# Retention into a gated FFN on one core: state casts two groups behind their block, one chunk's load behind the down weights, three blocks for chunks 4 to 7, and a longer run of half-column ups

## The chip, the cores and the metric

One core of a Trainium2 chip. The metric is the device time of one execution in microseconds (us). The fast executions of one kernel lie within 1% of each other, mostly within 0.7%; a few fall in a slower state, and they are left out. The kernel before took 236.76 us (median of 3, 236.72 to 236.99). Kernels are timed in rounds beside the kernel before, in sessions, each on one chip of its own.

## The reference, cut to what matters

```python
# retention: 4 batches, 8 heads, 768 tokens, head size 64; a decay gamma per head
state = gamma * state + outer(k[t], v[t])
y[t]  = scale * q[t] @ state
x     = y as 3072 tokens x 512
# gated FFN, d_ff = 1536
out = (sigmoid(x @ w_gate) * (x @ w_val)) @ w_out
```

The kernel cuts each batch into six chunks of 128 tokens (24 chunks in all) and the tokens of the FFN into six tiles of 512, which are four chunks each.

## The kernel before

TensorE (PE) is fed from one program order. The FFN of a tile is a list of groups: twelve `up` groups (gate and value matmuls, 512 columns), then eight half `down` groups. `plan` puts retention work between the groups: `step_t` transposes a chunk, `block(done, new)` finishes two chunks and starts two. In the code, `kn`, `qn` and `vf` are the loaded k, q and v of a chunk, `zbd` is the state in bf16, and `wg`, `wv` and `wo` are the gate, value and down weights. A bank is one of the seven PSUM buffers that PE's results go to; the program reuses it when another engine has read it out. "First columns" below are the first matmuls on columns 256 to 511 of tile 1.

```python
pf = ctx.enter_context(tc.tile_pool(name="pf", bufs=7, space=bass.MemoryType.PSUM))   # rotating banks
...
def state_sum(g):                       # g, g + 1: VectorE sums, then the casts on ScalarE
    ...
        nc.vector.tensor_tensor(new_za(g), za[g - 1], z[:, 0], op=ALU.add)
        state_out(g, za[g])             # two ScalarE copies: fp32 state to bf16 zbd
    if c + 1 < NCH - 1:
        nc.vector.tensor_tensor(new_za(g + 1), za[g], z[:, 1], op=ALU.add)
        state_out(g + 1, za[g + 1])

def step_t(g):
    transposes(g)                       # PE needs kn, qn; ScalarE copies the bank out
    scale_v(g, nc.vector)               # needs vf

def block(done, new):
    ...
    for g in olds: inter(g)             # PE: y from the state (needs zbd of g - 1)
    for g in news: scores(g)            # PE: two PSUM banks per chunk
    for g in olds: intra(g)             # PE: y from the masked scores
    ...                                 # PE: state(g) of the new chunks
    for g in olds: y_out(g)             # VectorE: y * decay -> xT, which the ups read
    for g in news: masks(g)             # VectorE: two masks per chunk free its score banks
    if news:
        state_sum(new)

def down(t, sm, part):
    ...
    ob = ffn.tile([128, D_MODEL], F32, tag="ob", name="ob")     # the pool has 3 buffers
    nc.scalar.copy(ob, o)
    nc.sync.dma_start(out=out[row:row + 128, :], in_=ob)
...
load_chunk(4)
for s in range(4): load_out(s)          # down weights
for g in range(5, 8): load_chunk(g)
...
plan = {
    0: [(4, step_t, 4), (10, step_t, 5), (11, block, None, 4), (11, step_t, 6), (13, step_t, 7), (14, block, 4, 6)],
    1: [(2, step_t, 8), (5, step_t, 9), (7, block, 6, 8), (12, step_t, 10), (14, step_t, 11), (15, block, 8, 10),
        (20, block, 10, None)],
    ...
}
# tile 1: eight ups on columns 0..255 (chunks 4, 5), then these ups' columns 256..511 (chunks 6, 7)
groups[:8] = [lambda n1=n1: up(1, n1, 0, 256) for n1 in range(8)]
groups[8:8] = [lambda n1=n1: up_columns(1, range(n1, n1 + 2), 256, 512) for n1 in range(0, 8, 2)]
```

Of the kernel before, what the change touches and what calls it, by code (L numbers as in the profile page):

```python
# [17 lines left out]
def kernel(  # L18
# [15 lines left out]
    NCH = S // C  # L34
# [25 lines left out]
    def load_v(g, eng):  # L60
        vf[g] = ld.tile([C, H, D], F32, tag="vf", name="vf", bufs=8)
        eng.dma_start(out=vf[g], in_=src(v, g))  # L62

    def load_kq(g):
        kn[g] = ld.tile([C, H, D], BF16, tag="kn", name="kn")
        qn[g] = ld.tile([C, H, D], BF16, tag="qn", name="qn")
        nc.gpsimd.dma_start(out=kn[g], in_=src(k, g))  # L67
        nc.gpsimd.dma_start(out=qn[g], in_=src(q, g))  # L68

    def load_chunk(g):  # L70
        load_kq(g)
        load_v(g, nc.gpsimd)
# [64 lines left out]
    zz, za = {}, {}  # L137
# [34 lines left out]
    def scores(g):  # L172
        t = qkT[g]
        sc[g] = (bank([128, NP, C]), bank([128, NP, C]))
        for p in range(NP):
            for i in range(2):
                half = slice(i * D, (i + 1) * D)
                nc.tensor.matmul(sc[g][i][:, p, :], t[half, p, :], t[half, NP + p, :], start=True, stop=True)  # L178
# [7 lines left out]
    def inter(g):  # L186
        y[g] = bank([128, NP, C])
        if g % NCH > 0:
            for p in range(NP):
                nc.tensor.matmul(y[g][:, p, :], zbd[(g - 1) % 4][:, p, :], qkT[g][:, NP + p, :],  # L190
                                 start=(p == 0), stop=False, skip_group_check=True)

    def state(g, to, start, stop=True):
        for p in range(NP):
            for i in range(2):
                nc.tensor.matmul(to[i * D:(i + 1) * D, p, :], kn[g][:, 2 * p + i, :], vs[g][:, 2 * p + i, :],
                                 start=start, stop=stop, skip_group_check=True)

    def state_out(g, z):
        for i in range(2):  # L200
            half = slice(i * D, (i + 1) * D)
            nc.scalar.copy(zbd[g % 4][half, :, half], z[half])  # L202
# [11 lines left out]
    def new_za(g):  # L214
        za[g] = at.tile([128, NP, D], F32, tag="za", name="za", bufs=3)
        return za[g]

    def state_sum(g):
        c = g % NCH
        z = zz[g]  # L220
        if c == 0:
            state_out(g, z[:, 0])
            nc.vector.tensor_copy(new_za(g), z[:, 0])
        else:
            nc.vector.tensor_tensor(new_za(g), za[g - 1], z[:, 0], op=ALU.add)  # L225
            state_out(g, za[g])
        if c + 1 < NCH - 1:
            nc.vector.tensor_tensor(new_za(g + 1), za[g], z[:, 1], op=ALU.add)
            state_out(g + 1, za[g + 1])

    def intra(g):
        first = g % NCH == 0
        for p in range(NP):
            for i, st in enumerate((stA[g], stB[g])):
                nc.tensor.matmul(y[g][i * D:(i + 1) * D, p, :], vs[g][:, 2 * p + i, :], st[:, p, :],  # L235
                                 start=(first and p == 0), stop=True, skip_group_check=True)

    def y_out(g):
        c = g % NCH
        if g % 4 == 0:  # L240
            xT[g // 4] = at.tile([128, NP, 512], BF16, tag="xT", name="xT")
        col = (g % 4) * C
        nc.vector.tensor_tensor(xT[g // 4][:, :, col:col + C], y[g], taby[:, :, c * C:(c + 1) * C], op=ALU.mult)  # L243
# [5 lines left out]
    def block(done, new):  # L249

        olds = [] if done is None else [done, done + 1]
        news = [] if new is None else [new, new + 1]
        for g in olds:
            inter(g)
        for g in news:
            scores(g)
        for g in olds:
            intra(g)
        if news:
            zz[new] = pz.tile([128, 2, NP, D], F32, tag="z", name="z")  # L260
            for i, g in enumerate(news):
                if g % NCH < NCH - 1:
                    state(g, zz[new][:, i], True)
        for g in olds:
            y_out(g)
        for g in news:
            masks(g)
        if news:
            state_sum(new)


# [2 lines left out]
    def up(t, n1, lo=0, hi=512):  # L274
        if t not in hT:
            hT[t] = ffn.tile([128, NFF, 512], BF16, tag="hT", name="hT", bufs=2)
        ps = []
        for w in (wg, wv):
            u = bank([128, 512])
            for kk in range(KT):  # L280
                nc.tensor.matmul(u[:, lo:hi], w[:, kk, n1 * 128:(n1 + 1) * 128], xT[t][:, kk, lo:hi],  # L281
                                 start=(kk == 0), stop=(kk == KT - 1))
            ps.append(u)
        gs = ffn.tile([128, 512], F32, tag="gs", name="gs")
        nc.scalar.activation(gs[:, lo:hi], ps[0][:, lo:hi], AX.Sigmoid)  # L285
        nc.vector.tensor_tensor(hT[t][:, n1, lo:hi], gs[:, lo:hi], ps[1][:, lo:hi], op=ALU.mult)  # L286

    def up_columns(t, n1s, lo, hi):
        n = hi - lo
        ps = []  # L290
        for w in (wg, wv):
            u = bank([128, 512])
            for i, n1 in enumerate(n1s):
                for kk in range(KT):
                    nc.tensor.matmul(u[:, i * n:(i + 1) * n], w[:, kk, n1 * 128:(n1 + 1) * 128], xT[t][:, kk, lo:hi],  # L295
                                     start=(kk == 0), stop=(kk == KT - 1))
            ps.append(u[:, :len(n1s) * n])
        gs = ffn.tile([128, 512], F32, tag="gs", name="gs")
        g = gs[:, :len(n1s) * n]
        nc.scalar.activation(g, ps[0], AX.Sigmoid)  # L300
        nc.vector.tensor_tensor(hT[t][:, n1s[0]:n1s[-1] + 1, lo:hi], g.rearrange("p (i n) -> p i n", n=n),
                                ps[1].rearrange("p (i n) -> p i n", n=n), op=ALU.mult)
# [55 lines left out]
    for s in range(2, NFF // 2):  # L358
        load_gate_val(s)
    extend_taby(512, 768)  # L360
    load_chunk(4)
    for s in range(4):
        load_out(s)
    for g in range(5, 8):
        load_chunk(g)
    keep_on(8)
    scores(0)
# [45 lines left out]
    def downs(t):  # L413
        return [lambda sm=sm, i=i: down(t, sm, i) for sm in range(4) for i in range(2)]

    plan = {
        0: [(4, step_t, 4), (10, step_t, 5), (11, block, None, 4), (11, step_t, 6), (13, step_t, 7), (14, block, 4, 6)],
        1: [(2, step_t, 8), (5, step_t, 9), (7, block, 6, 8), (12, step_t, 10), (14, step_t, 11), (15, block, 8, 10),
            (20, block, 10, None)],
        2: [(1, block, None, 12), (7, block, 12, 14), (15, block, 14, 16)],  # L420
        3: [(6, block, 16, 18), (15, block, 18, 20)],
        4: [(6, block, 20, 22), (14, block, 22, None)],
        5: [],
    }
    for t in range(NT):
        groups = ups(t) + downs(t)
        if t == NT - 1:
            groups[-2:] = [lambda: last_down(t)]
        if t == 0:
            groups = groups[4:]  # L430
            for g in range(8, 12):
                load_chunk(g)
        if t == 1:
            groups[:8] = [lambda n1=n1: up(1, n1, 0, 256) for n1 in range(8)]
            groups[8:8] = [lambda n1=n1: up_columns(1, range(n1, n1 + 2), 256, 512) for n1 in range(0, 8, 2)]
            for g in range(12, 16):
                load_chunk(g)
        if t == 2:
            scale_v(14, nc.gpsimd)
            scale_v(15, nc.gpsimd)  # L440
            load_chunk(18)
            scale_v(16, nc.gpsimd)
            scale_v(17, nc.gpsimd)
            load_chunk(19)
        if t == 3:
            for g in range(18, 22):
                scale_v(g, nc.gpsimd)
            load_chunk(22)
            load_chunk(23)
            scale_v(22, nc.gpsimd)  # L450
            scale_v(23, nc.gpsimd)
        for i, group in enumerate(groups):
            if i == len(groups) - 9:
                for g in range(4 * t + 8, 4 * t + 12):
                    if XBAR <= g < NG:
                        xbar(g)
            if t == 1 and i == len(groups) - 4:
                scale_v(12, nc.gpsimd)
                scale_v(13, nc.gpsimd)
                load_chunk(16)  # L460
                load_chunk(17)
            if t == 2 and i == len(groups) - 4:
                load_chunk(20)
                load_chunk(21)
            group()
            for at_group, step, *g in plan[t]:
                if at_group == i:
                    step(*g)
# [30 lines left out]
```

## Time and profile before

| view of the kernel before | reading |
|---|---|
| span of the profiled run | 235.7 us, PE busy 224.2 |
| VectorE (DVE), ScalarE (ACT) busy | 109.6 and 90.1 us |

The prediction shows four waits of PE, which it calls A to D. What stood behind the longest of them, C, is this stretch of the DVE timeline (start, length, engine, line, operation, count, idle before and what ended it):

```profile
55.15 1.29 DVE L243 TENSOR_TENSOR xT<-ff,taby 128x512 bf16<-128x512 f32 x2 [1.54 <-PE ff L235]
56.36 0.68 DVE L183 TENSOR_TENSOR stA<-ff,causal 128x512 bf16<-128x512 f32 x1
...
58.75 0.41 DVE L223 COPY za<-z 128x256 f32<-128x256 f32 x1
59.20 0.42 DVE L228 TENSOR_TENSOR za<-za,z 128x256 f32<-128x256 f32 x1
```

The block of chunks 4 and 6 gives DVE two y products, four masks and two sums, 4.5 us of work. The casts on ACT need the sums, which come last, and were put into ACT's queue at the block itself, so everything ACT owed PE stood behind them until 60.5 us.

### The profile page before, as it was taken

Reading aid. Unit: us, or ns where it says so; the run is one execution under the profiler, and the core shown is the slowest. Engines: PE = TensorE matmul, PEld = TensorE weight load, DVE = VectorE, ACT = ScalarE, POOL = GpSimd, SP = SyncE. Lnnn points to the kernel's source line nnn. Section 1 sums busy time; section 2 is a strip of 40 time slices with the busy share of each in tenths; the row PEclk is TensorE's granted clock in tenths of the full one; section 3 lists DMA queues with packets and bytes.
Section 4 is the critical chain, followed back from the end, with each engine's and each line's share of the span. In section 5 each row is a group of like instructions: output and inputs, shape, how many; then the busy total and the mean of one; then the engine's idle time right before and its main releaser. Section 6 shows DMA issues by size and latency. Waiting matters only on the chain.

```text
span 235.7 us, 4436 instructions
## 1 busy us (share of the span) xinstructions
PE 224.2 (95%) x1786; PEld 124.5 (53%) x1786; DVE 109.6 (46%) x200; ACT 90.1 (38%) x176; POOL 92.3 (39%) x111
## 2 busy tenths in 40 slices
PE   6879999899789999999999999999999999999994
PEld 6655644357678555444545445445445444444444
DVE  4566444077676473075844335735345722234301
ACT  8755334253726423245061432420632521333211
POOL 8999766588888543395013730000000000000000
PEclk9999999999999999999999999999999999999999
DMA  8999999999999999999999994002200001200022
GB/s 145 183 185 165 197 205 205 192 241 215 197 196 137 107 110 144 211 140 107 94 125 135 149 213 86 0 1 92 90 0 3 0 19 72 89 0 0 0 92 89
DMA packets 77556, 27.29 MB, mean 116 GB/s; under 512 B 65056, under 2 KB 73120, under 8 KB 77536
## 3 DMA queue, kind: packets, MB, share of 16 engines
q0 software_dynamic: 57616, 16.78, 81.3%
q1 hardware_dynamic: 19776, 10.16, 23.7%
q8 instruction: 14, 0.23, 0.4%
q10 hardware_dynamic: 144, 0.07, 0.1%
q14 instruction: 6, 0.05, 0.1%
HBM read 28.31 MB, written 6.29 MB: 147 GB/s over the span
## 4 chain that ended last, share of the span: by engine, by line
PE 77%; DMA 9%; POOL 8%; DVE 2%; issue 1%; ACT 0%; POOLq 0%; DVEq 0%
PE ff L281 40%; PE ff L312 24%; DMA wo<-in_moe_w_out_dram 5%; DMA wg<-in_moe_w_gate_dram 5%; PE ff L295 3%; PE ff L178 2%; PE ff L235 2%; PE ff L190 2%; POOL wg L81 2%; POOL wv L81 2%; PE ff L149 2%; POOL vf L62 1%; PE ff L332 1%; POOL qn L68 1%; POOL vs L169 1%
## 5 line engine op out<-in xcount | busy, mean ns | idle before, releaser
L286 DVE TENSOR_TENSOR hT<-gs,ff 128x512 bf16<-128x512 f32 (+2 forms) x72 | 45.7, 649 | 72.6 <-PE ff L281 57.4
L281 PE MATMUL ff<-xT,wg 128*128 128x512 bf16 (+2 forms) x288 | 69.7, 365 | 0.7 <-DVE xT L243 0.7
L281 PE MATMUL ff<-xT,wv 128*128 128x512 bf16 (+2 forms) x288 | 69.7, 365 | 0.0
L312 PE MATMUL ff<-wo,hT 128*128 128x512 bf16 x276 | 62.1, 380 | 1.2 <-DMA wo<-in_moe_w_out_dram 1.2
L285 ACT ACTIVATE gs<-ff 128x512 f32<-128x512 f32 (+2 forms) x72 | 39.5, 569 | 44.0 <-PE ff L281 43.5
L281 PEld LDWEIGHTS <-wv 128*128 128x128 bf16 x288 | 28.1, 98 | 29.9 <-DMA wv<-in_moe_w_val_dram 0.3
L312 PEld LDWEIGHTS <-hT 128*128 128x128 bf16 x276 | 26.4, 98 | 32.2 <-issue 1.6
L281 PEld LDWEIGHTS <-wg 128*128 128x128 bf16 x288 | 27.4, 98 | 28.3 <-issue 0.7
L317 ACT COPY ob<-ff 128x512 f32<-128x512 f32 x23 | 13.4, 585 | 38.3 <-PE ff L312 33.9
L243 DVE TENSOR_TENSOR xT<-ff,taby 128x512 bf16<-128x512 f32 x24 | 15.6, 687 | 24.9 <-PE ff L235 24.9
L202 ACT CAST zbd<-za 64x256 bf16<-64x256 f32 x26 | 10.5, 403 | 43.4 <-DVE za L225 33.9
L169 POOL TENSOR_TENSOR vs<-vf,tabv 128x512 bf16<-128x512 f32 x14 | 14.7, 1056 | 31.3 <-PE ff L281 12.9
L62 POOL DMA_DIRECT2D vf<-in_v_dram x23 | 21.1, 916 | 6.8 <-DMA kn<-in_k_dram 2.3
L67 POOL DMA_DIRECT2D kn<-in_k_dram x23 | 21.0, 914 | 3.6 <-DMA wo<-in_moe_w_out_dram 1.4
L68 POOL DMA_DIRECT2D qn<-in_q_dram x23 | 20.5, 890 | 3.1 <-DMA wo<-in_moe_w_out_dram 2.2
L183 DVE TENSOR_TENSOR stA<-ff,causal 128x512 bf16<-128x512 f32 x24 | 16.4, 682 | 3.4 <-PE ff L178 3.3
L184 DVE TENSOR_TENSOR stB<-ff,causal 128x512 bf16<-128x512 f32 x24 | 16.3, 681 | 0.0
L169 DVE TENSOR_TENSOR vs<-vf,tabv 128x512 bf16<-128x512 f32 x10 | 7.4, 736 | 7.6 <-DMA vf<-in_v_dram 7.6
L151 ACT ACTIVATE qkT<-ff 128x1024 bf16<-128x1024 bf16 x8 | 8.2, 1030 | 4.4 <-PE ff L149 4.3
L324 PE MATMUL ff<-ident 128*128 128x128 bf16 x82 | 7.3, 254 | 1.6 <-POOL ident masks.py:199 1.6
L235 PE MATMUL ff<-stA,vs 128*64 128x128 bf16 x96 | 8.2, 222 | 0.5 <-DVE stA L183 0.5
L235 PE MATMUL ff<-stB,vs 128*64 128x128 bf16 x96 | 7.9, 222 | 0.4 <-DVE stB L184 0.4
(62 smaller groups left out, 138.2 us busy)
## 6 DMA issues: line engine op xcount, KB each, us to landing
vf<-in_v_dram POOLq DMA_DIRECT2D x23, 256.0 KB, 7.9
out_dram<-ob SPq DMA_DIRECT2D x23, 256.0 KB, 3.3
kn<-in_k_dram POOLq DMA_DIRECT2D x23, 128.0 KB, 7.9
qn<-in_q_dram POOLq DMA_DIRECT2D x23, 128.0 KB, 7.8
wg<-in_moe_w_gate_dram POOLq DMA_DIRECT2D x6, 256.0 KB, 7.3
wv<-in_moe_w_val_dram POOLq DMA_DIRECT2D x6, 256.0 KB, 7.8
wo<-in_moe_w_out_dram POOLq DMA_DIRECT2D x4, 384.0 KB, 10.4
kf<-in_k_dram SPq DMA_DIRECT2D x1, 256.0 KB, 3.2
```

The lines of the kernel that those rows point to most:

```text
L62: eng.dma_start(out=vf[g], in_=src(v, g))
L67: nc.gpsimd.dma_start(out=kn[g], in_=src(k, g))
L68: nc.gpsimd.dma_start(out=qn[g], in_=src(q, g))
L169: eng.tensor_tensor(vs[g], vf[g], tabv[:, g % NCH, :].unsqueeze(2).to_broadcast([C, H, D]), op=ALU.mult)
L183: nc.vector.tensor_tensor(stA[g], sc[g][0], causal4, op=ALU.mult)
L184: nc.vector.tensor_tensor(stB[g], sc[g][1], causal4, op=ALU.mult)
L235: nc.tensor.matmul(y[g][i * D:(i + 1) * D, p, :], vs[g][:, 2 * p + i, :], st[:, p, :], start=(first and p == 0), stop=True, skip_group_che ...
L243: nc.vector.tensor_tensor(xT[g // 4][:, :, col:col + C], y[g], taby[:, :, c * C:(c + 1) * C], op=ALU.mult)
L281: nc.tensor.matmul(u[:, lo:hi], w[:, kk, n1 * 128:(n1 + 1) * 128], xT[t][:, kk, lo:hi], start=(kk == 0), stop=(kk == KT - 1))
L285: nc.scalar.activation(gs[:, lo:hi], ps[0][:, lo:hi], AX.Sigmoid)
L286: nc.vector.tensor_tensor(hT[t][:, n1, lo:hi], gs[:, lo:hi], ps[1][:, lo:hi], op=ALU.mult)
L312: nc.tensor.matmul(o, hT[t][:, n1, sm * 128:(sm + 1) * 128], wo[:, n1, :], start=(n1 == 0), stop=(n1 == NFF - 1))
```

## The change

The intent: keep ACT from standing at casts whose sums are not made yet; have the down weights land before they are wanted; push chunks 4 to 7 back to where their loads have landed; and put two more groups between the y products of chunks 6 and 7 and the first matmuls that read them.

```diff
 def state_sum(g):
-            state_out(g, z[:, 0])            # ... and the two other state_out calls
+    def casts(g):                            # now entries of the plan, two groups later (those of chunk 4: right behind the block)
+        for i in range(g, g + 2):
+            if i % NCH < NCH - 1:
+                state_out(i, za[i])
 def block(done, new):
+        if news and not olds:
+            state_sum(new)                   # a block that only starts chunks: sum before masks
         for g in news:
             masks(g)
-        if news:
+        if news and olds:
             state_sum(new)
-    load_chunk(4)
     for s in range(4):
         load_out(s)
-    for g in range(5, 8):
+    for g in range(4, 8):
         load_chunk(g)
 plan
-        0: [(4, step_t, 4), (10, step_t, 5), (11, block, None, 4), (11, step_t, 6), (13, step_t, 7), (14, block, 4, 6)],
-        1: [(2, step_t, 8), (5, step_t, 9), (7, block, 6, 8), (12, step_t, 10), (14, step_t, 11), (15, block, 8, 10),
-            (20, block, 10, None)],
+        0: [(9, step_t, 4), (11, step_t, 5), (12, block, None, 4), (12, casts, 4), (13, step_t, 6), (14, block, 4, None)],
+        1: [(0, step_t, 7), (2, block, None, 6), (3, step_t, 8), (4, casts, 6), (5, step_t, 9), (7, block, 6, 8),
+            (9, casts, 8), (11, step_t, 10), (13, step_t, 11), (15, block, 8, 10), (17, casts, 10), (20, block, 10, None)],
 ...                                          # tiles 2 to 4: the same blocks (one a group later), with casts two groups behind
-            groups[:8] = ... range(8)        # half-column ups
+            groups[:10] = ... range(10)
```

More of the change, by code (lines that the diff above doesn't have):

```diff
@@ L225, in state_sum @@
             nc.vector.tensor_tensor(new_za(g), za[g - 1], z[:, 0], op=ALU.add)
-            state_out(g, za[g])
         if c + 1 < NCH - 1:
             nc.vector.tensor_tensor(new_za(g + 1), za[g], z[:, 1], op=ALU.add)
-            state_out(g + 1, za[g + 1])
+    def casts(g):
+        for i in range(g, g + 2):
+            if i % NCH < NCH - 1:
+                state_out(i, za[i])
     def intra(g):
@@ L416 @@
     plan = {
-        0: [(4, step_t, 4), (10, step_t, 5), (11, block, None, 4), (11, step_t, 6), (13, step_t, 7), (14, block, 4, 6)],
-        1: [(2, step_t, 8), (5, step_t, 9), (7, block, 6, 8), (12, step_t, 10), (14, step_t, 11), (15, block, 8, 10),
-            (20, block, 10, None)],
-        2: [(1, block, None, 12), (7, block, 12, 14), (15, block, 14, 16)],
-        3: [(6, block, 16, 18), (15, block, 18, 20)],
-        4: [(6, block, 20, 22), (14, block, 22, None)],
+        0: [(9, step_t, 4), (11, step_t, 5), (12, block, None, 4), (12, casts, 4), (13, step_t, 6), (14, block, 4, None)],
+        1: [(0, step_t, 7), (2, block, None, 6), (3, step_t, 8), (4, casts, 6), (5, step_t, 9), (7, block, 6, 8),
+            (9, casts, 8), (11, step_t, 10), (13, step_t, 11), (15, block, 8, 10), (17, casts, 10), (20, block, 10, None)],
+        2: [(1, block, None, 12), (3, casts, 12), (7, block, 12, 14), (9, casts, 14), (16, block, 14, 16), (18, casts, 16)],
+        3: [(6, block, 16, 18), (8, casts, 18), (15, block, 18, 20), (17, casts, 20)],
+        4: [(6, block, 20, 22), (8, casts, 22), (14, block, 22, None)],
         5: [],
@@ L433 @@
         if t == 1:
-            groups[:8] = [lambda n1=n1: up(1, n1, 0, 256) for n1 in range(8)]
-            groups[8:8] = [lambda n1=n1: up_columns(1, range(n1, n1 + 2), 256, 512) for n1 in range(0, 8, 2)]
+            groups[:10] = [lambda n1=n1: up(1, n1, 0, 256) for n1 in range(10)]
+            groups[10:10] = [lambda n1=n1: up_columns(1, range(n1, n1 + 2), 256, 512) for n1 in range(0, 10, 2)]
             for g in range(12, 16):
```

## The prediction

> **What bounds the kernel now.** First the page: engine shares and the clock row, to see which engine fills the span.
>
> ```profile
> span 235.7 us, 4436 instructions
> PE 224.2 (95%) x1786; PEld 124.5 (53%) x1786; DVE 109.6 (46%) x200; ACT 90.1 (38%) x176; POOL 92.3 (39%) x111
> ...
> PEclk9999999999999999999999999999999999999999
> ```
>
> TensorE (PE) is busy 95% of the span at full clock; every other engine is below half. So the change can only win time in which PE stands still: 235.7 - 224.2 = 11.5 us. The busy time by stretch puts 4.5 us of it before 17 us (start of the pipeline) and 3.0 us after the last matmul (the tail). The diff touches neither. The rest is in the waits of PE, read next (total, times, longest):
>
> ```profile
> PE ff L149 <- ACT ob L317: 1.6, 1, 1.6
> PE ff L312 <- DMA wo<-in_moe_w_out_dram: 1.2, 1, 1.2
> PE ff L295 <- DVE xT L243: 0.9, 1, 0.9
> ...
> PE ff L149 <- DMA qn<-in_q_dram: 0.4, 1, 0.4
> ```
>
> Four waits, each once. The timeline of PE says where (start, length, instructions, idle before):
>
> ```profile
> 34.42 0.39 PE L149 MATMUL ff<-ident,kn 128*128 128x128 bf16 x4
> 35.17 0.40 PE L149 MATMUL ff<-ident,qn 128*128 128x128 bf16 x4 [0.36 <-DMA qn<-in_q_dram]
> 35.41 1.03 PE L281 MATMUL ff<-xT,wg 128*128 128x512 bf16 x4
> ...
> 40.59 2.17 PE L312 MATMUL ff<-wo,hT 128*128 128x512 bf16 x9
> 43.92 2.10 PE L312 MATMUL ff<-wo,hT 128*128 128x512 bf16 x9 [1.16 <-DMA wo<-in_moe_w_out_dram]
> ...
> 58.94 0.60 PE L281 MATMUL ff<-xT,wv 128*128 128x256 bf16 x4
> 61.13 0.39 PE L149 MATMUL ff<-ident,kn 128*128 128x128 bf16 x4 [1.59 <-ACT ob L317]
> ...
> 67.73 0.42 PE L196 MATMUL z<-vs,kn 128*64 128x64 bf16 x16
> 69.06 1.03 PE L295 MATMUL ff<-xT,wg 128*128 128x256 bf16 x8 [0.91 <-DVE xT L243]
> ```
>
> The printed idle starts at a modelled end, so I count from start to start. **A**: transposes of chunk 4 take 35.41 - 34.42 = 0.99 against 0.44 for those at 61.13: 0.55 lost. **B**: nine down matmuls at 0.216 end their issue at 40.59 + 1.94 = 42.53; the next starts at 43.92: 1.39. **C**: 58.94 + 0.44 = 59.38, next at 61.13: 1.75. **D**: sixteen state matmuls take 0.25 in undisturbed blocks, 67.98, next at 69.06: 1.08. Sum 4.77 us. After 69 us no PE wait on another engine is listed.
>
> The cause of C is in the timeline of ScalarE (ACT):
>
> ```profile
> 59.65 0.82 ACT L202 CAST zbd<-za 64x256 bf16<-64x256 f32 x2 [3.35 <-DVE za L228]
> 60.49 0.58 ACT L317 COPY ob<-ff 128x512 f32<-128x512 f32 x1
> ```
>
> ACT stood 3.35 us at a state cast that needs VectorE's (DVE) sum, itself behind two y products and four masks. The copy that frees the PSUM bank for PE stood behind it.
>
> **What the Trainium skill says.** "Perfetto Trace Analysis", Tensor Engine Instruction: the profiler estimates a matmul's end, and ACT and DVE are strict FIFO. The trace agrees: the copy at 60.49 follows the cast at once, though its matmuls had long ended, and my start-to-start sum is 0.7 us more than the printed idle. "TensorE: Matmul & The Clock Gate", Back-to-back issue gap: N/2.4 + 2.5 ns, 216 ns for 512 columns; the chain's piece of 56 matmuls in 12.09 us gives 215.9. "DMA: Bandwidth & Descriptors", Two DMAs through the same engine are not ordered: within one queue descriptors start in order but are pipelined. The loads here do land in order of issue (last gate slice 32.10, last down slice 43.88, vf of chunk 5 at 47.06), so reordering issues reorders landings.
>
> **Part 1, chunk 4 behind the down weights.** Chunk 4's parts land at issue + landing time: kn 24.65 + 9.7 = 34.35, qn 25.60 + 9.5 = 35.1, vf 27.1 + 8.9 = 36.0. The queue delivers the four down slices from 36.0 to 43.88, 7.9 us, and the chunk took about 2.5 us from about 33.4. With total bytes unchanged the last slice now lands near 33.4 + 7.9 = 41.3 (estimate), then kn4 42.2, qn4 43.1, vf4 43.9; chunks 5 to 7 land as before (vf5 47.0, vf6 about 49.7, vf7 52.9). Chunk 4's transposes leave the ups, so the downs start at 40.59 - 0.99 = 39.60. The last slice is wanted 1.94 later, 41.54: B gone, A gone. The first two down groups (12 matmuls) end at 42.2, and there the transposes of chunk 4 now come: qn4 at 43.1 makes them end at 43.37 instead of 42.64. **New wait 0.75.**
>
> **Part 2, three blocks and later casts.** No matmul is added; the same state, score and y matmuls are moved. The masks of chunks 4 and 5 are done near 51.35 (state sum at 48.6, then 0.34 + 4 x 0.60 of DVE), PE wants them at 51.9. The block that finishes 4 and 5 has no scores or state, one down group of 1.30 follows, and the first half-column up wants both y products, 2 x 0.6 + 0.07 after the last y matmul (as 55.15 to 56.44 now): **new wait about 0.1**. PE reaches that up near 53.8. ACT has no cast in front of the bank copies there, so C goes. But chunks 6 and 7 get a block of their own two groups later (57.7), now with the state sum (0.8) ahead of the masks. Its four score banks come free at about 59.3, 59.9, 60.5 and 61.1 by DVE's pace of 0.60. There are seven rotating banks; two half-column ups with 0.44 a bank use the three free ones plus these four: PE wants them from 59.0 on and runs 59.35 to 61.63 instead of 59.0 to 60.8. **New wait about 0.85.**
>
> **Part 3, ten half-column groups.** The two added half-columns cost nothing as work: four matmuls of 256 take 0.437, so two halves equal one full up. They put 1.75 us between the block and the first columns that need chunks 6 and 7, so D's wait for y goes. But the block holds six of the seven banks: the third and fourth bank of these groups wait for the second y product and the first mask, 0.2 and 0.16, as do the first columns by 0.16. **About 0.5 of D's 1.08 stays.**
>
> **After 69 us** the moved casts change ACT's order only; PE had no wait there. One link worried me: out stores of tile 1 queue behind transposing loads on SyncE until 86.8, which do not move with PE, and ACT waited 4.16 us for such a store until 99.48. But the store was itself late because of a cast (ACT until 89.43); with block and cast a group earlier the store can go near 87, so I expect no new wait.
>
> **Sum.** Saved 0.55 + 1.39 + 1.75 + 1.08 = 4.77; new 0.75 + 0.1 + 0.85 + 0.5 = 2.2; net 2.57. The old blocks also show some 0.5 us of small start gaps between 46 and 57 us, of which perhaps 0.1 goes. 236.76 - 2.65 = **234.1 us**.
>
> **Rivals.** (1) All four waits vanish and nothing replaces them: 232.0. For it: DVE is at 46% and ACT at 38%. Against: in the block stretch 56 to 61 us DVE is busy 3.6 of 5.1 us, and bank release has its pace. (2) Chunks 4 to 7 become the bound: stores of the downs now share the DMA engines with them a microsecond or two earlier. A vf5 or vf6 one to two microseconds late blocks DVE's queue before state sum, masks and y products, and PE stops for it: 235 to 236. For it: PE's slack on the masks is only 0.5 us, and DVE already waited 5.5 us for vf5. (3) The time is given back in tile 2, because PE arrives earlier at loads that have not moved: up to 2.5 us, 236.5. Against: qkX loads were never waited for, and vf14 lands 93 for a use at 113. (4) The last slice of the down weights still comes late by up to 0.5: 234.5.
>
> **Range and chances.** The new waits carry the error: 0.3 to 1.3 for chunk 4, 0.6 to 1.8 for the banks. So 233.1 to 235.4 holds it 8 times in 10. Two per cent faster means below 232.0, where all four waits must vanish without any successor: 0.03. Slower by 2% needs a new stall of 7 us: 0.01.
>
> **What will show it.** Part 1: PE's wait on wo is gone or below 0.3; instead a wait on qn at about 42 to 43 us. Part 2: no wait on an ob copy near 60; the first half-column up starts near 53.8; PE waits for masks (L183, L184) near 59 to 61.5. Part 3: the first columns of tile 1 start near 67.7, two half-column groups after their block. PE's busy sum stays about 224 and the span shrinks by the lost idle. It is wrong if a vf load appears as DVE's long wait before the masks, if PE shows a wait after 69 us, or if the masks cost nothing.

## The result, and the profile after

The changed kernel took 234.43 us (median of 4, one of them slow; the fast ones 233.85 to 234.60) against 236.74 us for the kernel before in the same session; the median of the three fast runs is 234.26. The ratio is 0.9898, 95% interval 0.9868 to 0.9929. Ratios are over the fast runs; they differ from the quotient of the mean times by up to 0.0003. Page and waits of PE after (total, times, longest):

```profile
span 232.9 us, 4448 instructions
...
PE 222.9 (96%) x1781; PEld 125.5 (54%) x1802; DVE 110.0 (47%) x201; ACT 91.8 (39%) x177; POOL 92.2 (40%) x111
```

```profile
...
PE ff L285 <- DVE xT L245: 0.7, 1, 0.7
PE ff L285 <- DMA wv<-in_moe_w_val_dram: 0.6, 1, 0.6
...
PE ff L237 <- DVE stB L184: 0.4, 1, 0.4
```

All four waits of before are gone. The first and the last line shown lie before 17 us, in the start that both kernels share. This trace holds 1781 PE matmuls; the repeat below, with the same program, holds 1802 and 224.3 us busy, so the 222.9 is low by records that are missing. The wait on `wv` is at 22.3 us, also in a stretch that the change does not touch. Now the timeline of PE where the predicted new waits were to come:

```profile
22.32 0.82 PE L285 MATMUL ff<-xT,wv 128*128 128x384 bf16 x4 [0.56 <-DMA wv<-in_moe_w_val_dram]
...
42.92 0.39 PE L149 MATMUL ff<-ident,kn 128*128 128x128 bf16 x4
43.15 0.39 PE L149 MATMUL ff<-ident,qn 128*128 128x128 bf16 x4
43.37 2.75 PE L316 MATMUL ff<-wo,hT 128*128 128x512 bf16 x12
...
59.04 0.39 PE L149 MATMUL ff<-ident,kn 128*128 128x128 bf16 x4
...
59.48 0.60 PE L285 MATMUL ff<-xT,wg 128*128 128x256 bf16 x4
...
61.28 0.39 PE L149 MATMUL ff<-ident,kn 128*128 128x128 bf16 x4
...
63.55 0.39 PE L190 MATMUL ff<-qkT,zbd 128*128 128x128 bf16 x4
64.03 0.93 PE L178 MATMUL ff<-qkT 64*128 64x128 bf16 x16
```

Counted from start to start as in the prediction: the transposes of chunk 4 take 0.45, no wait. From 59.04 to 61.28 lie eight transposes (0.45) and two half-column ups (4 x 0.437), 2.20 in all; 2.24 passed, so the banks cost 0.04 and not 0.85. The first mask of this block was still running when the first of these ups began:

```profile
59.06 0.68 DVE L183 TENSOR_TENSOR stA<-ff,causal 128x512 bf16<-128x512 f32 x1
```

One reading of the prediction has to be put right before D is compared: in undisturbed blocks sixteen state matmuls take 0.35 us to the next instruction (55.10 to 55.45 in the kernel before); 0.25 is what eight take. So D was 0.98, not 1.08, and A to D sum to 4.67. In the changed kernel 0.10 of D is left: the ups between the block and the first columns take 1.85 in place of 1.75.

But the block at 63.55 loses time that was not predicted. Its sixteen score matmuls start 0.16 late (0.48 after 63.55, where 0.32 is undisturbed); they and the matmuls behind them take 0.31 longer; with 0.07 at the up before, 0.54. ACT shows why:

```profile
60.60 0.38 ACT L289 ACTIVATE gs<-ff 128x256 f32<-128x256 f32 x1
61.01 1.65 ACT L202 CAST zbd<-za 64x256 bf16<-64x256 f32 x4
62.68 0.38 ACT L289 ACTIVATE gs<-ff 128x256 f32<-128x256 f32 x1
62.96 1.02 ACT L151 ACTIVATE qkT<-ff 128x1024 bf16<-128x1024 bf16 x1
63.86 0.67 ACT L289 ACTIVATE gs<-ff 128x256 f32<-128x256 f32 x2
```

The four casts no longer wait, but they still take 1.65 us of ACT, in a stretch where ACT has no time to spare. The sigmoids and the transposed copy that the scores need come late.

### The profile page after: what moved, and what is told of

The parts are those of the page before. It is cut to its first block, busy times and chain, and to the rows that moved or that the text cites. A ratio compares the mean times of both kernels' runs of the same rounds, so it can differ in the third digit from the quotient of the medians.

```text
span 232.9 us, 4448 instructions
## 1 busy us (share of the span) xinstructions
PE 222.9 (96%) x1781; PEld 125.5 (54%) x1802; DVE 110.0 (47%) x201; ACT 91.8 (39%) x177; POOL 92.2 (40%) x111
## 4 chain that ended last, share of the span: by engine, by line
PE 84%; POOL 6%; DMA 3%; issue 2%; DVE 2%; ACT 1%; POOLq 0%
PE ff L285 46%; PE ff L316 25%; PE ff L299 5%; DMA wv<-in_moe_w_val_dram 3%; PE ff L237 2%; PE ff L178 2%; PE ff L190 2%; PE ff L149 1%; PE ff L336 1%; POOL qn L68 1%; POOL kn L67 1%; PE z L196 1%; POOL vf L62 1%; POOL vs L169 1%; POOL wg L81 1%
## 5 line engine op out<-in xcount | busy, mean ns | idle before, releaser
L285 PE MATMUL ff<-xT,wg 128*128 128x512 bf16 (+2 forms) x277 | 68.0, 361 | 1.4 <-DVE xT L245 0.7
L285 PE MATMUL ff<-xT,wv 128*128 128x512 bf16 (+2 forms) x287 | 68.6, 361 | 0.7 <-DMA wv<-in_moe_w_val_dram 0.6
L289 ACT ACTIVATE gs<-ff 128x512 f32<-128x512 f32 (+2 forms) x72 | 40.2, 562 | 68.0 <-PE ff L285 62.0
L316 PE MATMUL ff<-wo,hT 128*128 128x512 bf16 x267 | 61.1, 379 | 0.9 <-issue 0.5
L202 ACT CAST zbd<-za 64x256 bf16<-64x256 f32 x32 | 12.9, 403 | 8.6 <-DVE za L224 8.0
```

Of the source, the lines that this page charges most:

```text
L285: nc.tensor.matmul(u[:, lo:hi], w[:, kk, n1 * 128:(n1 + 1) * 128], xT[t][:, kk, lo:hi], start=(kk == 0), stop=(kk == KT - 1))
L289: nc.scalar.activation(gs[:, lo:hi], ps[0][:, lo:hi], AX.Sigmoid)
L316: nc.tensor.matmul(o, hT[t][:, n1, sm * 128:(sm + 1) * 128], wo[:, n1, :], start=(n1 == 0), stop=(n1 == NFF - 1))
```

## The experiments

The last row is the best version. "Fast mean" is the mean of the fast runs; "before" is the same for the kernel before in the same rounds, and each value of it is one session. Ratios of different sessions are compared below where there is nothing better; their intervals often overlap, and then the traces decide.

| kernel | fast mean us | before | ratio | 95% interval |
|---|---|---|---|---|
| loads alone | 237.21 | 236.91 | 1.0013 | 0.9989 to 1.0037 |
| casts alone | 235.03 | 236.91 | 0.9918 | 0.9892 to 0.9943 |
| loads and casts | 235.41 | 236.91 | 0.9934 | 0.9911 to 0.9957 |
| change with eight half columns | 234.59 | 236.91 | 0.9899 | 0.9875 to 0.9924 |
| change, again | 234.23 | 236.75 | 0.9893 | 0.9869 to 0.9918 |
| change with two merged blocks | 235.09 | 236.75 | 0.9927 | 0.9905 to 0.9950 |
| change, one cast later | 234.25 | 236.75 | 0.9894 | 0.9863 to 0.9925 |
| change, block 8/10 later | 234.44 | 236.75 | 0.9902 | 0.9870 to 0.9935 |
| change without load order | 235.13 | 236.88 | 0.9926 | 0.9902 to 0.9951 |
| change with four output buffers | 233.74 | 236.88 | 0.9867 | 0.9841 to 0.9894 |
| change, masks first | 234.37 | 236.47 | 0.9913 | 0.9889 to 0.9936 |
| all three repairs | 233.20 | 236.88 | 0.9842 | 0.9813 to 0.9870 |

**My theory**: the four waits were real and separate, each part of the change takes one or two away, and new, smaller waits at ACT and at loads give part back. **The rival**: the waits share a cause or hide one another, so that one part alone brings it all or none. All kernels gave correct results.

One count over the traces leaves the start out: from the first 512-column up (25.6 to 26.5 us) to the first down matmul of tile 2. It took 94.78 us before, 91.17 and 91.80 in the two profiles of the change, and 90.30 in the best version. What follows took 115.2 us in all fourteen profiles, so what the edits do to the time lies before that.

### Loads alone, on the kernel before

```diff
-    load_chunk(4)                    # now after load_out, as in the change
-        0: [(4, step_t, 4), (10, step_t, 5), ...
+        0: [(9, step_t, 4), (10, step_t, 5), ...
```

> The kernel before with the load order alone: chunk 4 behind the down weights, and its transposes moved from group 4 to group 9 of tile 0. Casts, blocks and half columns as before. My account: waits A (0.55) and B (1.39) go, C and D stay; a wait for chunk 4's qn of 0 to 0.75 us may come. 1.2 to 1.9 us faster: ratio to before 0.992 to 0.995. Rival (the loads do not matter, PE only reaches the cast-blocked copy near 60 us earlier and waits there longer): ratio above 0.997 with wait C grown past 2.5 us.

Missed: no gain in time. The profile shows A and B gone, and C and D there in full (1.75 and 0.98). In place of A and B PE now meets chunk 5:

```profile
44.57 0.40 PE L149 MATMUL ff<-ident,kn 128*128 128x128 bf16 x4 [0.37 <-DMA kn<-in_k_dram]
45.39 0.40 PE L149 MATMUL ff<-ident,qn 128*128 128x128 bf16 x4 [0.42 <-DMA qn<-in_q_dram]
```

From start to start that is 0.53 + 0.58. Changing the order of loads hardly makes chunk 5 land earlier (its kn at 44.53 against 44.78); a PE that comes sooner waits for it, unless chunk 5's transposes move back too. The profiled run was still 0.7 us ahead at the first columns of tile 1 (68.37 against 69.06), while the timed runs show nothing. That stays open; the profiled run was the fastest of its six (236.79), and that of the kernel before (237.46) one of its slower ones.

### Casts alone, on the kernel before

```diff
 def state_sum(g):                    # without state_out, as in the change
-        1: [(2, step_t, 8), (5, step_t, 9), (7, block, 6, 8), ...
+        1: [(2, step_t, 8), (4, casts, 6), (5, step_t, 9), (7, block, 6, 8), (9, casts, 8), ...   # likewise elsewhere
```

> The kernel before with the state casts alone moved two groups behind their block; loads, blocks and half columns as before. If C is ACT's queue standing at a cast (my account), the wait of 1.75 us near 60 us drops below 0.7 and nothing else changes: about 1.1 to 1.6 us faster, ratio 0.993 to 0.996. Rival: the banks come free only at DVE's pace anyway (two y products, four masks, two sums = 4.5 us behind the block of chunks 4 and 6), then PE waits the same time for another releaser and the ratio is above 0.998.

It came out for my account, and a little better: 0.9918. The transposes of chunk 8 follow without a gap:

```profile
58.12 0.60 PE L283 MATMUL ff<-xT,wv 128*128 128x256 bf16 x4
58.56 0.39 PE L149 MATMUL ff<-ident,kn 128*128 128x128 bf16 x4
```

C was ACT's queue standing at a cast, not the drain of banks by DVE. B (1.13) and D (0.98) are still there. This part alone brings most of the whole gain.

### Loads and casts together

> Load order and moved casts together on the kernel before, with its two merged blocks and eight half-column groups. If the two parts are independent, the gains add: 2.3 to 3.3 us, ratio 0.986 to 0.990, which would be as good as the whole change or better. If the three blocks are needed for the casts to pay, the gain stays near that of the loads alone, ratio 0.992 to 0.995.

The edit is the sum of the two above. 0.9934 is not better than the casts alone, so the gains do not add: PE again waits for chunk 5 (0.47 and 0.57 at 44.6 and 45.4 us), and D stays.

### The change with two blocks in place of three

```diff
-  (13, step_t, 6), (14, block, 4, None)], 1: [(0, step_t, 7), (2, block, None, 6), ...
+  (13, step_t, 6), (14, step_t, 7), (14, block, 4, 6)], 1: [...
```

> The whole change but with chunks 6 and 7 scored in the block that finishes 4 and 5, as before, so two blocks in place of three. If the split is what lets PE run ahead of the late chunks 6 and 7, then the transposes of chunk 7 wait for its qn, DVE waits for its vf with the y products of 4 and 5 behind it, and the first half-column up starts 0.5 us or more after its turn, and six banks are then drained at DVE's pace: 0.8 to 1.6 us slower than the changed kernel, ratio to before 0.993 to 0.997. Rival: with the casts out of the way the split is worth nothing, ratio 0.990.

0.9927 against 0.9893 in the same rounds, 0.9 us slower, as expected. PE waits 0.79 for chunk 7's qn at 52.3 and 0.50 for its copy at 53.8; a further 0.35 at 42.8 is chunk 4's. DVE stands 1.48 us at the `vf` of chunk 7. The third block is there to let chunks 6 and 7 come after their loads.

### The change without its load order

```diff
+    load_chunk(4)
     for s in range(4):
         load_out(s)
-    for g in range(4, 8):
+    for g in range(5, 8):
```

> The changed kernel with the load order undone: chunk 4 ahead of the down weights as before, its transposes still behind the first two down groups. If the load order carries part of the gain, wait B returns in full (the last slice of the down weights near 43.0 to 43.9 for a want at 41.5: 1.1 to 2 us) and nothing later absorbs it, as chunks 5 to 7 are landed when PE comes later: ratio to before 0.994 to 0.997, 1.0 to 1.6 us slower than the changed kernel. Rival (the load order is worth nothing, as the run with it alone on the kernel before showed no gain): ratio 0.990.

0.9926, some 0.8 us slower than the change, less than expected and in another session. B is back:

```profile
42.77 0.81 PE L316 MATMUL ff<-wo,hT 128*128 128x512 bf16 x3 [1.13 <-DMA wo<-in_moe_w_out_dram]
```

From start to start B is 1.45, and the stretch is 1.45 longer than in the change's first profile (92.62 against 91.17), but only 0.82 longer than in the repeat, which loses 0.60 at a store (below); this kernel loses nothing there. Together with the first experiment: the load order is worth 0.8 us or more where the later chunks are pushed back, and no gain is resolved where they are not. The parts are not independent, so my theory holds for C; of A and B, removed alone, 1.11 of 1.94 came back as waits for chunk 5.

### The change with eight half columns

```diff
-            groups[:10] = ... range(10); groups[10:10] = ... range(0, 10, 2)
+            groups[:8]  = ... range(8);  groups[8:8]   = ... range(0, 8, 2)     # steps 10, 11 one group later
```

> The whole change except for the half columns: eight groups as before in place of ten. By the trace of the changed kernel the ten-group form starts its first columns with 0.1 us lost where the kernel before lost 1.08 (D). So 0.7 to 1.0 us slower than the whole change, ratio to before 0.993 to 0.995, with a PE wait on DVE xT of about 0.8 us at the first columns. Rival: D does not matter, because the time is taken back at another wait before tile 2: ratio 0.990 as the whole change.

The trace has D back in full:

```profile
65.94 0.81 PE L299 MATMUL ff<-xT,wg 128*128 128x256 bf16 x6 [0.91 <-DVE xT L245]
```

but the time does not show it: 0.9899, so the rival held. The repeat of the change, below, shows where the win of the ten groups is given back: in the ten-group form the block of chunks 8 and 10 lies before the last up of tile 1, and PE loses 0.31 at the first downs of tile 1 and 0.60 at the first block of tile 2. The eight-group form has neither. 0.98 against 0.10 + 0.31 + 0.60: even.

### The change again

> The changed kernel itself again, as a yardstick for its variants on the same chip. Its first profile lost 0.73 us at 22.3 us on a wait for a slice of the value weights, in a stretch that the change does not touch and that six other profiles do not show at more than 0.36. If that is a matter of the single run, this profile starts its first 512-column up near 25.8 and not 26.5 us, and PE then still finds chunk 4 landed at 42.2 us (no wait above 0.3), so that the span is about 232.2.

The profile starts its first 512-column up at 26.0 us, between the two values; the wait on the `wv` slice was 0.37 from start to start. So that wait comes and goes. Chunk 4 was there at 42.40. The span was not 232.2 but 232.9 again, because of a wait after 69 us that the first profile did not have:

```profile
96.97 0.59 ACT L321 COPY ob<-ff 128x512 f32<-128x512 f32 x1 [5.06 <-DMA out_dram<-ob]
```

```profile
97.27 0.55 PE L178 MATMUL ff<-qkX 64*128 64x128 bf16 x9
98.11 0.38 PE L178 MATMUL ff<-qkX 64*128 64x128 bf16 x7 [0.29 <-ACT gs L289]
```

ACT's fourth output copy of tile 1 waits for the first output buffer, whose store was issued at 85.69 right behind the last transposing load, and took until 97. The sigmoids behind that copy free their banks late, and PE stops in the scores of chunks 12 and 13: from start to start they take 1.15 in place of 0.55, 0.60 lost. Why this store takes 11 us, where the median store of the run takes 2.1, no experiment shows; in every profile it landed after the last transposing load, here 1.7 us after.

### One of the casts later

```diff
-  (4, casts, 6), (5, step_t, 9), (7, block, 6, 8), (9, casts, 8), ...
+  (4, cast_one, 6), (5, step_t, 9), (7, block, 6, 8), (8, cast_one, 7), (9, casts, 8), ...    # cast_one(g): state_out(g, za[g])
```

> The changed kernel with the cast of chunk 7's state moved from group 4 to group 8 of tile 1, so that only two casts in place of four (0.82 in place of 1.65 us) stand on ACT before the block of chunks 6 and 8. In the changed kernel's trace PE loses about 0.6 us at that block (63.1 to 64.9 us) behind ACT, which is late with its sigmoids and transposed copies after the casts. If the casts are the cause the loss falls below 0.2 and the kernel is 0.3 to 0.5 us faster than the changed one. Rival (DVE's masks are the cause): no difference.

In the trace the loss at the block of chunks 6 and 8 is gone: the scores run from 63.26 with no gap, and the first columns start at 66.48 against 67.03 in the repeat, after a start that agrees within 0.02 us.

```profile
63.26 0.62 PE L178 MATMUL ff<-qkT 64*128 64x128 bf16 x16
...
66.48 1.04 PE L302 MATMUL ff<-xT,wg 128*128 128x256 bf16 x8
```

So the casts were the cause. In time, 0.9894 against 0.9893: no gain is resolved, and its fast runs spread from 233.1 to 235.3. The profiled run was 0.5 us shorter than the repeat's (232.4 against 232.9).

### Block of chunks 8 and 10 behind the last up

```diff
-  (15, block, 8, 10), (17, casts, 10), (20, block, 10, None)
+  (16, block, 8, 10), (18, casts, 10), (21, block, 10, None)
```

> The changed kernel with the block of chunks 8 and 10, its casts and the block that ends 10 one group later in tile 1 (16, 18 and 21 for 15, 17 and 20), so that the block again comes after the last up. In the changed kernel's trace the first downs of tile 1 wait 0.32 us for the last up's hT, which stands behind this block's products, masks and sum on DVE. Expected: that wait is gone, 0.3 us faster than the changed kernel; rival: another wait takes its place in tile 2, no difference.

The wait at the first downs is gone, and the rival is right: the wait at the stores takes its place and more.

```profile
97.94 0.59 ACT L321 COPY ob<-ff 128x512 f32<-128x512 f32 x1 [6.24 <-DMA out_dram<-ob]
```

PE's scores there take 2.33 from start to start in place of 0.55, 1.78 lost. Nothing gained in time.

### Four output buffers

```diff
-        ob = ffn.tile([128, D_MODEL], F32, tag="ob", name="ob")
+        ob = ffn.tile([128, D_MODEL], F32, tag="ob", name="ob", bufs=4)
```

> The changed kernel with four output buffers in place of three. In four profiles of the changed kernel and its variants ACT's fourth copy of tile 1 stands until about 96.4 to 97.9 us for the first store of the tile, which was issued near 86 us behind the last transposing load, at a time that does not move with PE; PE then loses 0.45 (changed kernel, again) to 1.7 us (block one group later) at the scores of chunks 12 and 13. With a fourth buffer no copy waits for that store: PE's loss at 97 to 99 us falls below 0.15, 0.3 to 0.5 us faster than the changed kernel, ratio 0.987 to 0.988. Rival (the loss moves on into tile 2): no difference.

0.9867: about 0.6 us faster than the change by the ratios, which come from two sessions and whose intervals overlap; the stretch is 0.63 shorter than in the repeat (91.17 against 91.80). PE passes the scores of chunks 12 and 13 in one piece:

```profile
96.96 0.62 PE L178 MATMUL ff<-qkX 64*128 64x128 bf16 x16
97.51 0.44 PE L196 MATMUL z<-vs,kn 128*64 128x64 bf16 x16
```

### Masks first

```diff
-        if news and not olds:
-            state_sum(new)
         for g in news:
             masks(g)
-        if news and olds:
+        if news:
```

> The changed kernel with the masks ahead of the state sum also in a block that only starts chunks, as the kernel before had it. The prediction held that the sum in front of the masks delays the release of the score banks and costs PE up to 0.85 us near 59 to 61.5; the changed kernel's trace shows no such loss above 0.1. If the sum-first order still pays, it is by the casts: with masks first the sum of chunks 6 and 7 comes 2.4 us later, near 61.5 us, ACT stands at the cast of group 4 with two sigmoids and a transposed copy behind it, and PE's loss at the block of chunks 6 and 8 grows from 0.6 to over 1.2 us: 0.5 to 1.5 us slower than the changed kernel, ratio to before 0.992 to 0.996. If neither order matters, ratio 0.989; if the prediction's bank pace was right, faster, below 0.987.

0.9913: not resolved from the change. The trace shows no loss at 59 to 61 us (0.00) and, against my expectation, hardly a larger one at the next block (0.61 against 0.54): the masks now start at 57.62, as soon as the scores are there, and the sums end at 60.89, just as ACT reaches the casts. The order of sum and masks did not matter in either direction.

### All three repairs

The edit is the sum of the last cast, block and buffer edits.

> Three repairs of the changed kernel together: one of the two casts before the block of chunks 6 and 8 moved behind it (0.6 us at 63 to 65), the block of 8 and 10 behind the last up of tile 1 (0.3 us at 84.6), and the fourth output buffer (0.5 us at 98, 1.7 with the later block). If the later loss is a wall at the stores that took back what the first two gained, all three together give 1.0 to 1.4 us over the changed kernel: ratio to before 0.984 to 0.986, span near 231.5. Rival: 0.989 as each alone.

0.9842, or 3.7 us faster than the kernel before and about 1.2 faster than the change. PE now waits on nothing between 17.4 us and the tail:

```profile
PE ff L331 <- POOL ident masks.py:199: 1.6, 1, 1.6
PE ff L288 <- DVE xT L248: 0.7, 1, 0.7
PE ff L240 <- DVE stB L184: 0.4, 1, 0.4
PE ff L158 <- ACT qn L360: 0.4, 1, 0.4
```

It is also 0.54 us faster than the four buffers alone, timed in the same rounds, and every fast run of the one (232.82 to 233.53) is below every run of the other (233.64 to 233.92). So two repairs that show nothing in time alone do count, taken together, once the store is out of the way. This is the best version here.

## Why the prediction was right or wrong

The time was right: 234.1 predicted, 234.43 measured (234.26 for the fast runs), inside 233.1 to 235.4. The account behind it was right for what goes and wrong for what comes: of the three signs of being wrong that the prediction names, two plainly appeared, a PE wait after 69 us and masks that cost nothing.

**The four waits**: right. A, B and C are gone, and 0.10 of D is left; only D was read 0.10 too large. The cause of C, a cast at the head of ACT's queue, is shown by the run with the casts alone.

**Part 1, chunk 4**: the last slice of the down weights came in time, at 40.89 in the first profile against 41.3 reckoned. The term "new wait 0.75" was too large. Chunk 4 was there when PE came at 42.1 to 42.9 us in most profiles; the largest loss was 0.44 (with the later block). My landing time of 43.1 for qn was reckoned from one run's queue; it landed at 42.55 in the first profile, and between 41.93 and 42.89 in all that have this load order. What I did not say is that the load order pays only because chunks 5 to 7 are pushed back as well.

**Part 2, banks**: the wait on the y products came out at 0.01 against 0.1. The step that failed is "its four score banks come free ... PE runs 59.35 to 61.63": I took the seven banks to be reused strictly in turn. The masks came at the pace of 0.60 that I had reckoned; the first one ends at 59.74, the second at 60.34. But the first of the two ups starts at 59.48, and the semaphores in the trace have it wait for ACT and not for DVE; so it did not take the score bank that I gave it. Of its four bank uses only the second and the third wait for DVE, and only the third is held, until the second mask has ended. Measured 0.04 in place of 0.85, and masks first changes nothing. In its place stands a wait that I had not seen: the moved casts at group 4 take ACT 1.65 us just before the next block, 0.54 lost. I had asked only whether a cast would wait, not what it occupies. "No matmul is added" was no proof either that a third block is free: from start to start the blocks of chunks 4 to 7 take 0.89 + 1.11 + 1.02 = 3.02 us in the repeat, and 0.89 + 1.97 = 2.86 before, 0.16 more.

**Part 3**: 0.10 stays, not 0.5; the 0.5 rested on the same order of banks.

**After 69 us**: "I expect no new wait" was wrong, and rival (3) holds in part. The last up's hT stands behind the earlier block on DVE (0.32), and the first store of tile 1 does not move with PE (0 in the first profile, 0.60 in the repeat). I had looked at the right link and dismissed it because the cast ahead of it had gone; what was left is the store's own 10 to 12 us in the change's two profiles and the later-block one, with only three buffers.

**The sum**: 4.77 saved and 2.2 given back was predicted. For the repeat's profile 0.01 + 0.04 + 0.16 + 0.54 + 0.10 + 0.31 + 0.60 = 1.76 are found given back: 4.67 - 1.76 = 2.91, and the stretch from the first 512-column up to tile 2's downs shrank by 2.98 (94.78 to 91.80). That the net agreed with the prediction was luck: errors of both signs met. Of the new waits that were predicted 2.05 too much was charged, and 1.6 came from places that were not seen.

## What to carry to other kernels

Put an instruction into an in-order engine's queue where its input is ready, and count also the time it takes there: a cast that no longer waits can still be in front of what the bound engine needs. A reordered load may only move a wait, as here, unless the uses of the loads behind it are moved too. When a repair shows nothing, look in the trace for the next thing that does not move with the bound engine (here a store and its buffer), lift it, and try the repair again.

## What the Trainium skill lacked or had wrong

- "TensorE: Matmul & The Clock Gate", Back-to-back issue gap, gives about 131 ns per 512-column and 81 ns per 128-column matmul for sustained streams of weight load and matmul, and calls N/2.4 + 2.5 ns the gap of an isolated one. Here sustained streams with a weight load for every matmul run at that formula: 56 matmuls of 512 columns in 12.09 us are 215.9 ns each, and eight 128-column transposes in 0.45 us are about 56 ns each. The point is on this section alone.
- "DMA: Bandwidth & Descriptors", Two DMAs through the same engine are not ordered, warns that order of issue is no guarantee of landing. It does not say how far landing times vary between runs of one kernel: here the same slice of value weights cost PE from nothing to 0.73 us at about 22 us, and the first 512-column up started between 25.57 and 26.52 us across the profiles, behind the same PE instructions in all of them.
